# Decode attention, forward and backward: the sums for o and dq with N=512 in four column groups, and the row-broadcast of q in the score bank

## The chip, the cores and the metric

The kernel runs on one core of a Trainium2 chip. The metric is the device time in microseconds; the time before is the median of 12 runs. A profile is one execution, recorded by the hardware profiler. The engines are TensorE (PE; its weight loads are listed as PEld), VectorE (DVE), ScalarE (ACT), GpSimd (POOL) and SyncE (SP); sixteen DMA engines move data between HBM and the on-chip memory (SBUF). Matmul results land in PSUM[...].

## The reference

It is single-query softmax attention for B x H = 64 heads, with Sk = 8192 keys and D = 128, in bf16, together with its gradients:

```python
scores = jnp.einsum("bhqd,bhkd->bhqk", q, k) * scale
p = _softmax(scores, axis=-1)
return jnp.einsum("bhqk,bhkd->bhqd", p, v)
...
_out, _vjp = jax.vjp(_f, q, k, v)
_grads = _vjp(grad_out)
return (_out0, *[jnp.asarray(_g) for _g in _grads])
```

For one head, with s = K q, p = softmax(s) and dp = V g (g is the incoming gradient): o = sum of p_n V_n; dS = p (dp - sum p dp); dq = scale x sum of dS_n K_n; dK_n = scale x dS_n q; dV_n = p_n g. K, V, dK and dV have 2 MB a head each, so a head reads 4 MB and writes 4 MB; o and dq are single rows.

## The kernel before, in words

The 8192 rows of a head are laid out as 128 partitions times NT = 64 row tiles. A loop runs over slots, `SL` = 8 a head and two heads more than there are (L345). In slots 0 to 3 of head i the chunks of 16 tiles of K are transposed on TensorE (`transpose_chunk`, L139) into a PSUM tile `tp` of two banks, and ScalarE copies them to SBUF as `ev` (L147); in slots 4 to 7 the same is done with V. One slot later `score_chunk` (L150) multiplies each transposed tile, as weights, with the column of q (into `sw`) or of g (into `dpw`): 16 matmuls with one column each.

Beside that runs the head before. In slots 0 to 3 `acc_o` (L270) sums E x V: 64 matmuls, each with one column of E as weights and one 128x128 tile of V as the moving operand, into one row `oacc`. In slots 4 to 7 `acc_dq` (L286) sums dS x K: 64 matmuls, each with a tile of K as weights and one column of dS as the moving operand, into one column `qacc`. ScalarE scales the sums (`end_o` L302, `end_dq` L310). VectorE makes dV in slots 2 to 5 and dK in slots 6, 7, 0 and 1 (`outer`, L318: four products of 128x2048 for each), and POOL stores each of them with a DMA (L337) once it is whole.

The softmax's small steps are spread over the slots: maximum along a partition (`max_part`, slot 4), over partitions by a transpose (`max_all`, 5), spread back by a matmul and exponentiated (`max_spread` and `expo`, 6), sum of p x dp (`weigh`, slot 0 of the next head), normalisers, dS and the factors of the outer products (`normalise`, 1). `broadcast` (L108, slot 1) repeats the row of q and that of g over 128 partitions with a matmul and copies the result to `qb`.

Every compute instruction is pinned to program order on its engine. K and V tiles have six buffers of 2 MB (`kvp`). A load is issued by SP (L101, L106) when the sums over the tile that held the buffer are done; outputs have four buffers. PSUM: `tp` 2 x 2 banks, `sw` and `dpw` a bank each, and two banks of the pool `ps_m` that `qbp`, `oacc` and `qacc` share in turn.

Of the kernel before, what the change touches and what calls it, by code (L numbers as in the profile page):

```python
# [8 lines left out]
ACT = mybir.ActivationFunctionType  # L9
ALU = mybir.AluOpType  # L10
AX = mybir.AxisListType
BF16 = mybir.dt.bfloat16
F32 = mybir.dt.float32

CH = 16


@with_exitstack
def kernel(
# [11 lines left out]
    nc = tc.nc  # L31
    B, H, Sq, D = q.shape
    Sk = k.shape[2]
    P = nc.NUM_PARTITIONS
    assert Sq == 1 and D == P
    BH = B * H
    assert BH <= P
    NT = Sk // P
    assert NT * P == Sk and NT == 4 * CH
    NCH = NT // CH  # L40
    SL = 2 * NCH
    scale = float(D) ** -0.5

    load_eng = nc.sync
    store_eng = nc.gpsimd
    pin = tc.keep_in_program_order

    const = ctx.enter_context(tc.tile_pool(name="const", bufs=1))
    kvp = ctx.enter_context(tc.tile_pool(name="kv", bufs=6))
    evp = ctx.enter_context(tc.tile_pool(name="ev", bufs=3))  # L50
    work = ctx.enter_context(tc.tile_pool(name="work", bufs=3))
    outp = ctx.enter_context(tc.tile_pool(name="outp", bufs=4))
    ps_tp = ctx.enter_context(tc.tile_pool(name="ps_tp", bufs=2, space=bass.MemoryType.PSUM))
    ps_sdp = ctx.enter_context(tc.tile_pool(name="ps_sdp", bufs=1, space=bass.MemoryType.PSUM))
    ps_m = ctx.enter_context(tc.tile_pool(name="ps_m", bufs=2, space=bass.MemoryType.PSUM))


    qd_nat = const.tile([BH, 2, D], BF16)
# [9 lines left out]
    ident_bf = const.tile([P, P], BF16)  # L68
# [6 lines left out]

    qdT = const.tile([P, 2, BH], BF16)
    for w in range(2):
        tps = ps_m.tile([P, BH], BF16, tag="m")
        nc.tensor.transpose(tps[:], qd_nat[:, w, :], ident_bf[:BH, :BH])
        nc.vector.tensor_copy(out=qdT[:, w, :], in_=tps[:])  # L80


    dqT = const.tile([P, BH], BF16)
    o_all = const.tile([1, BH, D], BF16)

    class Head:
        pass

    heads = [Head() for _ in range(BH)]

# [17 lines left out]
    def broadcast(i):  # L108

        h = heads[i]  # L110
        qbp = ps_m.tile([P, 2, D], F32, tag="m", name="qbp")
        pin(
            nc.tensor.matmul(  # L113
                qbp[:],
                lhsT=ident_bf[:BH, i : i + 1].to_broadcast([BH, P]),
                rhs=qd_nat[:],
                start=True,
                stop=True,
            )
        )  # L120
        h.qb = work.tile([P, 2, D], BF16, tag="qb", name="qb")
        pin(nc.vector.tensor_copy(out=h.qb[:], in_=qbp[:]))  # L122

    def begin_s(i):

        h = heads[i]
        sw = ps_sdp.tile([P, NT + P + 1], F32, tag="s", name="sw")
        h.s = sw[:, 0:NT]
        h.mT = sw[0:1, NT : NT + P]
        h.mb = sw[:, NT + P : NT + P + 1]  # L130
# [56 lines left out]
    def expo(i):  # L187
        h = heads[i]
        h.E_f = work.tile([P, NT], F32, tag="E_f", name="E_f")
        h.ld = work.tile([P, 2], F32, tag="ld", name="ld")  # L190
        pin(
            nc.scalar.activation(  # L192
                out=h.E_f[:],
                in_=h.s,
                func=ACT.Exp,
                bias=h.negm[:],
                scale=scale,
                accum_out=h.ld[:, 0:1],
            )
        )  # L200
        h.E_bf = work.tile([P, NT], BF16, tag="E_bf", name="E_bf")
        pin(nc.vector.tensor_copy(out=h.E_bf[:], in_=h.E_f[:]))  # L202

    def weigh(i):
        h = heads[i]
# [14 lines left out]
    def normalise(i):  # L220
        h = heads[i]
        pin(nc.tensor.matmul(h.lsum, lhsT=ones_f[:], rhs=h.ld[:], start=True, stop=True))  # L222
        h.rl = work.tile([P, 1], F32, tag="rl", name="rl")
        pin(nc.vector.reciprocal(out=h.rl[:], in_=h.lsum[:, 0:1]))
        negdelta = work.tile([P, 1], F32, tag="negdelta", name="negdelta")
        pin(
            nc.vector.tensor_scalar(
                out=negdelta[:],
                in0=h.lsum[:, 1:2],
                scalar1=h.rl[:],  # L230
                scalar2=-1.0,
                op0=ALU.mult,
                op1=ALU.mult,
            )
        )
        h.rls = work.tile([P, 1], F32, tag="rls", name="rls")
        pin(
            nc.vector.tensor_scalar(
                out=h.rls[:], in0=h.rl[:], scalar1=scale, scalar2=None, op0=ALU.mult
            )  # L240
        )
        dSu = work.tile([P, NT], F32, tag="dSu", name="dSu")
        pin(
            nc.vector.scalar_tensor_tensor(
                out=dSu[:],
                in0=h.dp,
                scalar=negdelta[:],
                in1=h.E_f[:],
                op0=ALU.add,
                op1=ALU.mult,  # L250
            )
        )
        h.dS_bf = work.tile([P, NT], BF16, tag="dS_bf", name="dS_bf")
        pin(nc.vector.tensor_copy(out=h.dS_bf[:], in_=dSu[:]))

        h.pair = []
        for src, norm, tag in ((dSu, h.rls, "ds2"), (h.E_f, h.rl, "p2")):
            d = work.tile([P, NT, 2], BF16, tag=tag, name="pair")
            pin(
                nc.vector.tensor_scalar(  # L260
                    out=d[:],
                    in0=src[:].unsqueeze(2).to_broadcast([P, NT, 2]),
                    scalar1=norm[:],
                    scalar2=None,
                    op0=ALU.mult,
                )
            )
            h.pair.append(d)

    def acc_o(i, c):  # L270

        h = heads[i]
        if c == 0:
            h.oacc = ps_m.tile([1, D], F32, tag="m", name="oacc")
        for n in range(c * CH, (c + 1) * CH):
            pin(
                nc.tensor.matmul(  # L277
                    h.oacc[:],
                    lhsT=h.E_bf[:, n : n + 1],
                    rhs=h.vt[:, n, :],  # L280
                    start=(n == 0),
                    stop=(n == NT - 1),
                )
            )

    def acc_dq(i, c):  # L286

        h = heads[i]
        if c == 0:
            h.qacc = ps_m.tile([P, 1], F32, tag="m", name="qacc")  # L290
        for n in range(c * CH, (c + 1) * CH):
            pin(
                nc.tensor.matmul(  # L293
                    h.qacc[:],
                    lhsT=h.kt[:, n, :],
                    rhs=h.dS_bf[:, n : n + 1],
                    start=(n == 0),
                    stop=(n == NT - 1),
                )
            )  # L300

    def end_o(i):  # L302
        h = heads[i]
        pin(
            nc.scalar.activation(  # L305
                out=o_all[:, i, :], in_=h.oacc[:], func=ACT.Copy, scale=h.rl[0:1, :]
            )
        )

    def end_dq(i):  # L310
        h = heads[i]
        pin(
            nc.scalar.activation(
                out=dqT[:, i : i + 1], in_=h.qacc[:], func=ACT.Copy, scale=h.rls[:]
            )
        )

# [27 lines left out]
    for g in range(SL * (BH + 2)):  # L345
        i, s = divmod(g, SL)
        live = i < BH
        one = 0 <= i - 1 < BH
        two = 0 <= i - 2 < BH

        if s == NCH and 1 <= i and i + 2 < BH:
            load_k(i + 2)
        if s == 0 and 2 <= i and i + 1 < BH:
            load_v(i + 1)
        if live:
            if s == 1:
                begin_s(i)
                broadcast(i)
            if s == NCH + 1:
                begin_dp(i)  # L360
            ev = transpose_chunk(i, s)

        if live and s == 5:
            max_all(i)
        if one and s == 1:
            normalise(i - 1)
        if one:
            if s < NCH:
                acc_o(i - 1, s)
            else:  # L370
                acc_dq(i - 1, s - NCH)
        if live and s == 6:
            max_spread(i)
            expo(i)
        if prev is not None:
            score_chunk(*prev)
        prev = (i, s, ev) if live else None
        if live and s == 4:
            max_part(i)
        if one and s == 0:  # L380
            weigh(i - 1)
        if one and s == NCH - 1:
            end_o(i - 1)
        if one and s == SL - 1:
            end_dq(i - 1)
        if one and 2 <= s < 6:
            outer(i - 1, 1, s - 2)
        if one and s >= 6:
            outer(i - 1, 0, s - 6)
        if two and s < 2:  # L390
            outer(i - 2, 0, s + 2)

    tps = ps_m.tile([BH, P], BF16, tag="m")
    nc.tensor.transpose(tps[:], dqT[:], ident_bf[:])
    dqn = const.tile([BH, D], BF16)
    nc.vector.tensor_copy(out=dqn[:], in_=tps[:])
    load_eng.dma_start(out=out_1.rearrange("b h s d -> (b h s) d"), in_=dqn[:])
    load_eng.dma_start(out=out_0.rearrange("b h s d -> s (b h) d"), in_=o_all[:])


# [28 lines left out]
```

## Time and profile before

| | us |
|---|---|
| median of 12 runs (lowest, highest) | 1329.43 (1322.1, 1336.16) |
| the profiled execution, as timed | 1329.01 |
| its span in the profile | 1327.2 |
| TensorE busy, of it the transposes (L145) | 1215.8, 603.1 |
| o sums (L277), dq sums (L293), TensorE | 298.6, 143.1 |
| ScalarE busy, of it the copies of transposes (L147) | 989.4, 946.1 |
| VectorE busy, of it the outer products (L325) | 744.7, 606.6 |
| a load of V, a store, from issue to landing (median) | 29.4, 26.8 |
| moved by the DMA engines | 540.37 MB, mean 407 GB/s |

Busy time is the time in which an engine executed at least one instruction; since matmuls are pipelined, the mean of one (231 ns for an o matmul) is longer than the distance between two. A timeline line reads: start, duration, engine, line, operation, output <- inputs, shape, number of instructions, and in brackets the idle time before it with what ended it. A line of the table by stage reads: stretch and length, then busy time (and number of instructions) of PE, PEld, DVE, ACT and POOL, the granted TensorE clock, the busy share of the DMA engines, and GB/s. A wait line reads: who waited at which line, for whom at which line, total, times and longest, all in us.

### The profile page before, as it was taken

The page shows a single profiled execution, that of the slowest core. Times are in us where ns is not written, and L with a number is a line of the kernel's source. Part 1 is how long each engine was busy: PE and PEld are TensorE (multiplying, and loading weights), DVE is VectorE, ACT ScalarE, POOL GpSimd, SP SyncE. Part 2 cuts the span into 40 slices and gives each one's busy share as a digit, 9 for nine tenths or more (in the row PEclk, how much of TensorE's full clock was granted, in tenths as well). Part 3 has the DMA queues.
Part 4 walks back from the last instruction along what each step waited for, and adds up shares of the span by engine and source line. Part 5 has one row for each costly group of instructions (what it writes and reads, how often), then busy time and mean ns, then how long its engine had stood idle before and what let it go on. Part 6 is the DMA issues. An engine that isn't in the chain of part 4 may idle for free.

```text
span 1327.2 us, 53368 instructions
## 1 busy us (share of the span) xinstructions
PE 1215.8 (92%) x24963; PEld 1133.3 (85%) x24963; DVE 744.7 (56%) x1412; ACT 989.4 (75%) x769; POOL 69.5 (5%) x136
## 2 busy tenths in 40 slices
PE   7998998899999999998999999999999999998993
PEld 6888897899898889988888888898888888888883
DVE  1555555565665665665565655655555556565655
ACT  7776777777777787877877778777677777776872
POOL 0000000000000000000000000000000000000000
PEclk9888989988989998998988989989789899898997
DMA  9999999999999999999999999999999999999976
GB/s 378 404 388 412 402 413 412 401 379 414 427 415 429 424 425 425 427 425 427 427 414 421 409 414 413 411 421 427 409 407 416 406 409 410 412 386 427 417 320 278
DMA packets 37760, 540.37 MB, mean 407 GB/s; under 512 B 4385, under 2 KB 4385, under 8 KB 4897
## 3 DMA queue, kind: packets, MB, share of 16 engines
q1 hardware_dynamic: 19106, 268.51, 49.1%
q0 software_dynamic: 18432, 268.44, 48.5%
q8 instruction: 195, 3.19, 0.9%
q14 instruction: 27, 0.22, 0.0%
HBM read 268.47 MB, written 268.47 MB: 405 GB/s over the span
## 4 chain that ended last, share of the span: by engine, by line
PE 63%; issue 28%; DMA 5%; POOL 1%; ACT 1%; DVE 0%; SPq 0%; POOLq 0%; ACTq 0%
PE tp L145 28%; PE oacc L277 15%; PE dpw L157 6%; PE sw L157 6%; PE qacc L293 5%; DMA kt<-in_k_dram 4%; POOL out_dram L337 1%; PE sw L179 1%; DMA vt<-in_v_dram 1%; PE qbp L113 1%; PE dpw L222 1%; ACT ev L147 1%; PE sw L173 0%; DVE ob L325 0%; SPq L96 0%
## 5 line engine op out<-in xcount | busy, mean ns | idle before, releaser
L147 ACT COPY ev<-tp 128x2048 bf16<-128x2048 bf16 x512 | 946.1, 1869 | 308.6 <-PE tp L145 304.9
L325 DVE TENSOR_TENSOR ob<-qb,pair 128x2048 bf16<-128x2048 bf16 x512 | 606.6, 1217 | 0.0
L145 PE MATMUL tp<-ident_bf,kt 128*128 128x128 bf16 x4096 | 310.1, 236 | 20.5 <-DMA kt<-in_k_dram 13.4
L145 PE MATMUL tp<-ident_bf,vt 128*128 128x128 bf16 x4096 | 293.0, 228 | 18.1 <-issue 16.7
L277 PE MATMUL oacc<-vt,E_bf 128*1 128x128 bf16 x4096 | 298.6, 231 | 4.2 <-issue 4.1
L157 PEld LDWEIGHTS <-ev 128*128 128x128 bf16 x8192 | 243.6, 97 | 64.9 <-issue 33.3
L145 PEld LDWEIGHTS <-kt 128*128 128x128 bf16 x4096 | 264.5, 106 | 31.5 <-DMA kt<-in_k_dram 14.5
L277 PEld LDWEIGHTS <-E_bf 128*1 128x1 bf16 x4096 | 247.3, 89 | 29.7 <-issue 12.9
L145 PEld LDWEIGHTS <-vt 128*128 128x128 bf16 x4096 | 248.5, 102 | 21.3 <-issue 19.5
L157 PE MATMUL dpw<-qdT,ev 128*128 128x1 bf16 x4096 | 145.4, 164 | 24.5 <-issue 23.1
L293 PE MATMUL qacc<-dS_bf,kt 128*128 128x1 bf16 x4096 | 143.1, 164 | 15.8 <-issue 15.8
L293 PEld LDWEIGHTS <-kt 128*128 128x128 bf16 x4096 | 136.5, 97 | 18.2 <-issue 17.3
L157 PE MATMUL sw<-qdT,ev 128*128 128x1 bf16 x4096 | 141.4, 164 | 3.3 <-issue 2.4
L337 POOL DMA_DIRECT2D out_dram<-ob x128 | 68.4, 534 | 1245.4 <-DVE ob L325 1241.4
L169 DVE TENSOR_REDUCE mp<-sw 128x1 f32<-128x64 f32 x64 | 14.4, 225 | 210.1 <-PE sw L157 210.1
L208 DVE CUSTOM_DVE_ANT_0 junk<-E_f,dpw 128x64 bf16<-128x64 f32 x64 | 14.2, 221 | 169.9 <-PE dpw L157 169.9
L202 DVE CAST E_bf<-E_f 128x64 bf16<-128x64 f32 x64 | 12.5, 195 | 84.1 <-ACT E_f L192 84.1
L182 DVE TENSOR_SCALAR negm<-sw 128x1 f32<-128x1 f32 x64 | 10.1, 159 | 85.0 <-PE sw L179 85.0
L122 DVE CAST qb<-qbp 128x256 bf16<-128x256 f32 x64 | 26.8, 418 | 4.3 <-PE qbp L113 4.3
L179 PE MATMUL sw<-gm,ones_f 1*128 1x1 f32 x128 | 26.1, 270 | 0.9 <-issue 0.9
L305 ACT ACTIVATE o_all<-oacc,rl 1x128 bf16<-1x128 f32 x64 | 22.7, 354 | 4.0 <-PE oacc L277 4.0
L192 ACT ACTIVATE E_f<-sw,negm 128x64 f32<-128x64 f32 x64 | 21.1, 329 | 3.1 <-DVE negm L182 3.0
(34 smaller groups left out, 268.4 us busy)
## 6 DMA issues: line engine op xcount, KB each, us to landing
out_dram<-ob POOLq DMA_DIRECT2D x128, 2048.0 KB, 26.8
vt<-in_v_dram SPq DMA_DIRECT2D x64, 2048.0 KB, 29.4
kt<-in_k_dram SPq DMA_DIRECT2D x63, 2048.0 KB, 27.7
kt<-in_k_dram SPq DMA_DIRECT2D x4, 512.0 KB, 5.3
qd_nat<-in_q_dram SPq DMA_DIRECT2D x1, 16.0 KB, 2.0
qd_nat<-in_grad_out_dram SPq DMA_DIRECT2D x1, 16.0 KB, 2.0
out_dram<-o_all SPq DMA_DIRECT2D x1, 16.0 KB
out_dram<-dqn SPq DMA_DIRECT2D x1, 16.0 KB, 7.2
```

The costliest lines, as they stand in the source:

```text
L122: pin(nc.vector.tensor_copy(out=h.qb[:], in_=qbp[:]))
L145: pin(nc.tensor.transpose(tp[:, t, :], src[:, n0 + t, :], ident_bf[:]))
L147: pin(nc.scalar.copy(out=ev[:], in_=tp[:]))
L157: nc.tensor.matmul(dst[:, n0 + t : n0 + t + 1], lhsT=ev[:, t, :], rhs=qdT[:, w, i : i + 1], start=True, stop=True,)
L169: pin(nc.vector.reduce_max(out=h.mp[:], in_=h.s, axis=AX.X))
L179: pin(nc.tensor.matmul(h.mb, lhsT=ones_f[0:1, :], rhs=h.gm[:], start=True, stop=True))
L192: nc.scalar.activation(out=h.E_f[:], in_=h.s, func=ACT.Exp, bias=h.negm[:], scale=scale, accum_out=h.ld[:, 0:1],)
L277: nc.tensor.matmul(h.oacc[:], lhsT=h.E_bf[:, n : n + 1], rhs=h.vt[:, n, :], start=(n == 0), stop=(n == NT - 1),)
L293: nc.tensor.matmul(h.qacc[:], lhsT=h.kt[:, n, :], rhs=h.dS_bf[:, n : n + 1], start=(n == 0), stop=(n == NT - 1),)
L305: nc.scalar.activation(out=o_all[:, i, :], in_=h.oacc[:], func=ACT.Copy, scale=h.rl[0:1, :])
L325: nc.vector.tensor_tensor(out=h.ob[:, n0 : n0 + CH, :].rearrange("p n (e t) -> p n e t", t=2), in0=h.qb[:, w, :] .rearrange("p (e t) -> p ...
L337: store_eng.dma_start(out=dst[i], in_=h.ob[:])
```

## The change

The sums for dq and o get one form, `acc(i, w, c)`: four row tiles are the moving operand of one matmul (128 x 512), with 32 neighbouring columns of dS or E as weights, of which the first four belong to these tiles. Its output is 32 partitions x 512 fp32. The four matmuls of a chunk write to the four blocks of 32 partitions of one bank, four column groups of the array. So 16 matmuls take the place of 64. In each block only row j of the j-th 128 columns (j from 0 to 3) is wanted. `pick` multiplies the bank by a mask `diag` on VectorE and adds the four parts; `join` adds up the 128 partitions with an fp32 matmul against ones, and ScalarE scales the column. The pick for o stands in slot 4, its join in slot 6; the pick for dq in slot 0 of the next head, its join in slot 2. E and dS are written to padded buffers of 92 columns, three of each, cleared once. o is now collected as columns and transposed at the end, as dq was.

`ps_m` now holds one bank for each of the two sums. The row-broadcast of q and g goes to the free part of the score bank `sw`, and is made in slot 0, ahead of the first transposes of K.

```diff
+QT = 4
+CW = 32
+NG = 4
...
-    ps_m = ctx.enter_context(tc.tile_pool(name="ps_m", bufs=2, space=bass.MemoryType.PSUM))
+    ps_m = ctx.enter_context(tc.tile_pool(name="ps_m", bufs=1, space=bass.MemoryType.PSUM))
...
+    groups = [g * P // NG for g in range(NG)]
+    diag = const.tile([P, QT, D], F32)
+    nc.vector.memset(diag[:], 0.0)
+    for g in groups:
+        nc.vector.tensor_copy(
+            out=diag[g : g + CW],
+            in_=ident_f[g : g + CW, g : g + QT].unsqueeze(2).to_broadcast([CW, QT, D]),
+        )
+
+    NW = NT + CW - QT
+    NBUF = 3
+    E_pads = [const.tile([P, NW], BF16, name=f"E_pad{j}") for j in range(NBUF)]
+    dS_pads = [const.tile([P, NW], BF16, name=f"dS_pad{j}") for j in range(NBUF)]
+    for t in E_pads + dS_pads:
+        nc.vector.memset(t[:], 0.0)
...
-        qbp = ps_m.tile([P, 2, D], F32, tag="m", name="qbp")
...
-                qbp[:],
+                h.qbp,
...
-        sw = ps_sdp.tile([P, NT + P + 1], F32, tag="s", name="sw")
+        sw = ps_sdp.tile([P, NT + P + 1 + 2 * D], F32, tag="s", name="sw")
+        h.qbp = sw[:, NT + P + 1 :].rearrange("p (w d) -> p w d", w=2)
...
-        h.E_bf = work.tile([P, NT], BF16, tag="E_bf", name="E_bf")
-        pin(nc.vector.tensor_copy(out=h.E_bf[:], in_=h.E_f[:]))
+        h.E_bf = E_pads[i % NBUF]
+        pin(nc.vector.tensor_copy(out=h.E_bf[:, 0:NT], in_=h.E_f[:]))
...
-    def acc_o(i, c):
-
-        h = heads[i]
+    def acc(i, w, c):
+
+        h = heads[i]
+        rows = h.vt if w else h.kt
+        wts = h.E_bf if w else h.dS_bf
         if c == 0:
-            h.oacc = ps_m.tile([1, D], F32, tag="m", name="oacc")
-        for n in range(c * CH, (c + 1) * CH):
+            h.acc[w] = ps_m.tile([P, QT * D], F32, tag=f"acc{w}", name="acc")
+        for m in range(CH // QT):
+            n0 = c * CH + m * QT
+            g = groups[m % NG]
             pin(
                 nc.tensor.matmul(
-                    h.oacc[:],
-                    lhsT=h.E_bf[:, n : n + 1],
-                    rhs=h.vt[:, n, :],
-                    start=(n == 0),
-                    stop=(n == NT - 1),
+                    h.acc[w][g : g + CW, :],
+                    lhsT=wts[:, n0 : n0 + CW],
+                    rhs=rows[:, n0 : n0 + QT, :].rearrange("p n d -> p (n d)"),
+                    start=(c == 0 and m < NG),
+                    stop=(c == NCH - 1 and m >= CH // QT - NG),
                 )
             )
...
+    def pick(i, w):
+
+        h = heads[i]
+        full = work.tile([P, QT, D], F32, tag="full", name="full")
+        h.sel = work.tile([P, D], F32, tag="sel", name="sel")
+        NR = P
+        pin(
+            nc.vector.tensor_tensor(
+                out=full[0:NR],
+                in0=h.acc[w][0:NR].rearrange("p (n d) -> p n d", n=QT),
+                in1=diag[0:NR],
+                op=ALU.mult,
+            )
+        )
+        pin(
+            nc.vector.reduce_sum(
+                out=h.sel[0:NR], in_=full[0:NR].rearrange("p n d -> p d n"), axis=AX.X
+            )
+        )
+
+    def join(i, w):
+
+        h = heads[i]
+        NR = P
+        pin(
+            nc.tensor.matmul(
+                h.acc[w][:, 0:1], lhsT=h.sel[0:NR], rhs=ones_f[0:NR, 0:1], start=True, stop=True
+            )
+        )
         pin(
             nc.scalar.activation(
-                out=o_all[:, i, :], in_=h.oacc[:], func=ACT.Copy, scale=h.rl[0:1, :]
-            )
-        )
...
+                out=(oT if w else dqT)[:, i : i + 1],
+                in_=h.acc[w][:, 0:1],
+                func=ACT.Copy,
+                scale=(h.rl if w else h.rls)[:],
             )
         )
...
-            if s == 1:
+            if s == 0:
                 begin_s(i)
                 broadcast(i)
...
-            if s < NCH:
-                acc_o(i - 1, s)
-            else:
-                acc_dq(i - 1, s - NCH)
+            acc(i - 1, 1 if s < NCH else 0, s % NCH)
+        if one and s == NCH + 2:
+            join(i - 1, 1)
+        if two and s == 2:
+            join(i - 2, 0)
...
-        if one and s == NCH - 1:
-            end_o(i - 1)
-        if one and s == SL - 1:
-            end_dq(i - 1)
+        if one and s == NCH:
+            pick(i - 1, 1)
+        if two and s == 0:
+            pick(i - 2, 0)
...
-    load_eng.dma_start(out=out_0.rearrange("b h s d -> s (b h) d"), in_=o_all[:])
+    for w, (src, dst, name) in enumerate(((dqT, out_1, "dqn"), (oT, out_0, "on"))):
+        tps = ps_m.tile([BH, P], BF16, tag=f"acc{w}", name="tps")
+        nc.tensor.transpose(tps[:], src[:], ident_bf[:])
+        nat = const.tile([BH, D], BF16, name=name)
+        nc.vector.tensor_copy(out=nat[:], in_=tps[:])
+        load_eng.dma_start(out=dst.rearrange("b h s d -> (b h s) d"), in_=nat[:])
```

More of the change, by code (lines that the diff above doesn't have):

```diff
@@ L77 @@
     for w in range(2):
-        tps = ps_m.tile([P, BH], BF16, tag="m")
+        tps = ps_m.tile([P, BH], BF16, tag=f"acc{w}", name="tps")
         nc.tensor.transpose(tps[:], qd_nat[:, w, :], ident_bf[:BH, :BH])
@@ L83, with __init__ @@
     dqT = const.tile([P, BH], BF16)
-    o_all = const.tile([1, BH, D], BF16)
+    oT = const.tile([P, BH], BF16)
+    groups = [g * P // NG for g in range(NG)]
[12 more added lines that the diff above has]
+        nc.vector.memset(t[:], 0.0)
     class Head:
-        pass
+        def __init__(self):
+            self.acc = [None, None]
     heads = [Head() for _ in range(BH)]
@@ L121, in broadcast @@
         h.qb = work.tile([P, 2, D], BF16, tag="qb", name="qb")
-        pin(nc.vector.tensor_copy(out=h.qb[:], in_=qbp[:]))
+        pin(nc.vector.tensor_copy(out=h.qb[:], in_=h.qbp))
     def begin_s(i):
         h = heads[i]
-        sw = ps_sdp.tile([P, NT + P + 1], F32, tag="s", name="sw")
+        sw = ps_sdp.tile([P, NT + P + 1 + 2 * D], F32, tag="s", name="sw")
+        h.qbp = sw[:, NT + P + 1 :].rearrange("p (w d) -> p w d", w=2)
         h.s = sw[:, 0:NT]
@@ L252, in normalise @@
         )
-        h.dS_bf = work.tile([P, NT], BF16, tag="dS_bf", name="dS_bf")
-        pin(nc.vector.tensor_copy(out=h.dS_bf[:], in_=dSu[:]))
+        h.dS_bf = dS_pads[i % NBUF]
+        pin(nc.vector.tensor_copy(out=h.dS_bf[:, 0:NT], in_=dSu[:]))
         h.pair = []
@@ L283, in acc_o @@
                 )
             )
-    def acc_dq(i, c):
+    def pick(i, w):
         h = heads[i]
[L289 to L298, printed above, removed]
-                )
-            )
@@ L302, in end_o @@
-    def end_o(i):
-        h = heads[i]
+        full = work.tile([P, QT, D], F32, tag="full", name="full")
[7 more added lines that the diff above has]
+                op=ALU.mult,
+            )
+        )
[4 more added lines that the diff above has]
+        )
@@ L304, in end_o @@
+    def join(i, w):
+        h = heads[i]
+        NR = P
[4 more added lines that the diff above has]
+        )
         pin(
             nc.scalar.activation(
-                out=o_all[:, i, :], in_=h.oacc[:], func=ACT.Copy, scale=h.rl[0:1, :]
-            )
-        )
-    def end_dq(i):
-        h = heads[i]
-        pin(
-            nc.scalar.activation(
-                out=dqT[:, i : i + 1], in_=h.qacc[:], func=ACT.Copy, scale=h.rls[:]
+                out=(oT if w else dqT)[:, i : i + 1],
+                in_=h.acc[w][:, 0:1],
+                func=ACT.Copy,
+                scale=(h.rl if w else h.rls)[:],
@@ L391 @@
             outer(i - 2, 0, s + 2)
[L393 to L397, printed above, removed]
-    load_eng.dma_start(out=out_0.rearrange("b h s d -> s (b h) d"), in_=o_all[:])
+    for w, (src, dst, name) in enumerate(((dqT, out_1, "dqn"), (oT, out_0, "on"))):
[4 more added lines that the diff above has]
+        load_eng.dma_start(out=dst.rearrange("b h s d -> (b h s) d"), in_=nat[:])
 _INS = ['q', 'k', 'v', 'grad_out']
```

## The prediction

> **What bounds the kernel now.** I read the page first: busy times, transfer rate by slice, DMA queues, the chain that ended last.
>
> ```profile
> PE 1215.8 (92%) x24963; PEld 1133.3 (85%) x24963; DVE 744.7 (56%) x1412; ACT 989.4 (75%) x769; POOL 69.5 (5%) x136
> ...
> GB/s 378 404 388 412 402 413 412 401 379 414 427 415 429 424 425 425 427 425 427 427 414 421 409 414 413 411 421 427 409 407 416 406 409 410 412 386 427 417 320 278
> ...
> q1 hardware_dynamic: 19106, 268.51, 49.1%
> q0 software_dynamic: 18432, 268.44, 48.5%
> ...
> PE 63%; issue 28%; DMA 5%; POOL 1%; ACT 1%; DVE 0%; SPq 0%; POOLq 0%; ACTq 0%
> ```
>
> Two things look full at once. TensorE is busy 92% of the span and holds 63% of the chain. But loads (q1) and stores (q0) together took 97.6% of sixteen DMA engines' span, and for ten slices the rate stood at 424 to 429 GB/s as at a ceiling. Which of the two is the limit decides everything, so next the SP queue's own waits and the busy time by stage.
>
> ```profile
> SPq L101 <- PE oacc L277: 690.3, 61, 16.7
> SPq L106 <- PE qacc L293: 502.8, 61, 10.6
> ...
> 60.00:100.00 40.00, 37.63 (x737) 34.86 (x734) 20.89 (x42) 29.58 (x22) 2.13 (x4) 0.85 0.99 392
> ...
> 500.00:600.00 100.00, 97.67 (x2049) 91.64 (x2046) 60.79 (x114) 80.92 (x63) 5.86 (x11) 0.91 1.01 426
> ...
> 1000.00:1100.00 100.00, 92.39 (x1917) 86.39 (x1913) 56.07 (x105) 76.87 (x60) 5.33 (x10) 0.91 1.00 406
> ```
>
> Loads are issued when the sums over V and K free a buffer: that speaks for TensorE. But the last columns (granted clock, DMA share, GB/s) show the engines' share at 0.99 to 1.01 in every stretch. So I looked at when each of the sixteen engines reports its part of a transfer done; the trace has all sixteen marks of nearly every load. The last mark came behind the fifteenth by this much:
>
> ```
> load landed at (us)   305  408  510  613  716  818  920  1023  1127  1230
> last behind 15th (us) 0.5  1.7  4.5  7.2  9.7 12.6 13.1  17.4  16.0  16.9
> ```
>
> The stores show the same ramp. **One DMA engine is slower than the other fifteen.** Nearly all their 16 KB packets take 0.611 us in the plateau; about one packet in sixteen takes 0.62 to 0.70 (by the packet rows around 1287 us, where that engine works alone: about 0.63 a load packet, 0.65 a store packet). A transfer is usable only when its last sixteenth is there, so this engine's pace counts. From 347 us, where its lag is near zero, to 1325 us, where it catches up at the last store, each engine moved 1521 packets: 978/1521 = 0.643 us. A load with a store is 16 packets, 10.3 us; a head (two of each) 20.6 us. Heads start 20.2 us apart on average over all 63 gaps. So from about 350 us on the kernel runs at the pace of one slow engine, and TensorE only looks like the limit: it fills its slack with half-clock stretches (granted clock 0.90). Before 350 us, with no lag, TensorE is the limit: the 527.3 packets of 4 to 347 us took 0.6505 each.
>
> **The change part by part.** One head of TensorE's work at full clock:
>
> ```profile
> 603.08 1.07 PE L145 MATMUL tp<-ident_bf,kt 128*128 128x128 bf16 x16 [0.67 <-DMA kt<-in_k_dram]
> ...
> 608.33 1.05 PE L145 MATMUL tp<-ident_bf,kt 128*128 128x128 bf16 x16
> 609.32 1.05 PE L277 MATMUL oacc<-vt,E_bf 128*1 128x128 bf16 x16
> 610.30 0.55 PE L157 MATMUL sw<-qdT,ev 128*128 128x1 bf16 x16
> 610.72 1.05 PE L145 MATMUL tp<-ident_bf,kt 128*128 128x128 bf16 x16
> ...
> 614.98 1.05 PE L145 MATMUL tp<-ident_bf,vt 128*128 128x128 bf16 x16
> 615.87 0.27 PE L173 MATMUL sw<-ident_f,mp 128*1 128x128 f32 x1
> 615.98 0.54 PE L293 MATMUL qacc<-dS_bf,kt 128*128 128x1 bf16 x16
> 616.38 0.54 PE L157 MATMUL dpw<-qdT,ev 128*128 128x1 bf16 x16
> 616.78 1.05 PE L145 MATMUL tp<-ident_bf,vt 128*128 128x128 bf16 x16
> ...
> 620.39 0.54 PE L157 MATMUL dpw<-qdT,ev 128*128 128x1 bf16 x16
> ```
>
> Start to start: sixteen transposes 0.89, sixteen o matmuls 0.98, sixteen dq matmuls 0.40, sixteen scores 0.41. The whole head runs from 603.08 to about 620.8: 17.7 us.
>
> *Removed:* 4 x 0.98 + 4 x 0.40 = 5.5 us a head.
>
> *Added, 32 matmuls with N=512.* No row has column groups. The nearest is the transposes' pace: 0.89/(16 x 128) = 0.435 ns a column, 0.22 us for 512. If four groups overlap fully, eight groups of four cost about 8 x 0.24 = 1.9 us a head. If nothing overlaps, not even the weight load (row L277: 89 ns for a one-column load), 32 x (0.22 + 0.09) = 10.0 us. The Trainium skill is on both sides. "TensorE: Matmul & The Clock Gate", section "Packing small matmuls — row/col tiling", gives 2.38 times for three column tiles at N=512: as an estimate 0.22 x 3/2.38 = 0.28 us a group, 2.2 us a head. It also says that a weight load is pulled ahead of a running matmul only where the row groups differ; here all use all 128 rows, which would mean 10.0. The trace weighs against that reading: the o matmuls, all rows too, come 61 ns apart (0.98/16), though a weight load (89) and 128 columns (56) make 145 one after the other. I take 2.2. "TensorEngine Tiling (Array Packing)", "Key Properties", speaks against the change: switching the tiling mode drains TensorE. Sixteen switches a head, at the 164 ns that one single-column matmul lasts (row L157), are up to 2.6 us more; no run here shows a switch, so zero to 2.6, and I take 1.3.
>
> *Added, two joins:* fp32 with 128x128 weights, as the L222 pair (0.34 us by its timeline row): 0.7 us a head. Bounds 0.4 and 0.8.
>
> TensorE sum: 17.7 - 5.5 + 2.2 + 1.3 + 0.7 = 16.4 us (14.8 to 23.5 between the ends), against 20.6 for the slow DMA engine. Throttled time comes on top, perhaps 1 to 2 us as now.
>
> *VectorE:* two picks a head, each 512 fp32 products out of PSUM and a reduction of 512. By rows L122 (256 elements, 418 ns) and L202 (64, 195 ns), 1.16 ns an element: 0.72 us and, from L169 (64, 225 ns), 0.75; 1.5 us a pick (1.2 to 1.6). 64 x 2.9 = 188 us, so VectorE goes from 745 to about 930 us, 70%. The o pick stands behind mp and ahead of an outer product and gm in VectorE's order; gm comes about 0.2 + 1.5 + 1.2 + 0.3 = 3.2 us after mp's scores, and TensorE asks for it (L179, behind join) about 3.1 us after them. Free, or a few tenths; uncovered it would be 1.5 us a head. Everything that TensorE has queued behind it, next the scores, would wait with it, and ScalarE's exponential too. The dq pick stands ahead of the reciprocal, which nothing needs until the dq sums three slots on.
>
> *The rest.* ScalarE's two small copies shrink from 354+273 to about 2 x 273 ns; it needs 8 x 1.87 + 1.1 = 16 us a head, inside 20.6. The broadcast moves to slot 0, before K is needed; its bank was last read in slot 6, and its cast only moves ahead of weigh (0.42 us): zero. The setup (a mask, six cleared buffers, some 5 us of VectorE, between nothing and 5) lies beside the first loads. TensorE's instructions fall by a quarter, so instruction fetches too (q8 has 0.9% of the engines): under 3 us, mostly on other engines. Loads and stores are the same; no queue gets another order. At the end three picks make the last store's issue 4 us later (1314.9 to about 1319), but the slow engine is busy with the store before it until 1321: zero.
>
> **Sum.** The slow engine has 2048 packets. About 57 are loads before any store (it has no lag until 41 us): 57 x 0.611 = 34.8. The others, 1991 x 0.643 = 1280.2. With 4 us ahead of the first and 2.2 behind the last: 1321.2 us of span, against 1327.2. So at most 6 us are to be won, all of it where TensorE is the limit now, before 350 us. I take three quarters: span 1322.7. The profiled execution took 1329.01, 1.8 over its span, and the median is 1329.43; so 1324.5 us, 0.37% less.
>
> **Rivals.** *A, the forecast*, 1324.5 (1318 to 1330): the slow engine sets the end. For it: lag ramp and pace. Against: it cannot be seen on the page.
> *B, TensorE is the limit or the slow pace comes from TensorE's load.* Then the plateau's 0.617 mean holds for all: 2048 x 0.617 = 1264, with 4 and 2.2 and some 20 us of a drained end: 1290, and 1.8: about 1292. For it: 63% of the chain, and SP's waits for TensorE. Against: the lag grows just where TensorE is quickest (500 to 600).
> *C, slower: column groups don't overlap and weight loads aren't pulled ahead.* The sums cost 10.0 us, TensorE 17.7 - 5.5 + 10.0 + 0.7 = 22.9, and with 64 x (22.9 - 20.6) = 147 us more the kernel takes about 1475; partial overlap ends anywhere between. It decides from the point where four matmuls take over 20.6 - 12.9 = 7.7 us a head, 0.96 us a group. For it: the row-group rule, the mode switch. Against: the 61 ns pace of the o matmuls.
>
> **Chances.** A 0.65, B 0.12, C 0.23. About 0.3% (4 us) is what a measurement can tell from no change. A's own spread gives faster 0.36, within 0.26, slower 0.03; B is faster; C is within 0.03, slower 0.20. Together 0.48, 0.29, 0.23. For 8 in 10 the range takes A, a quarter of B and half of C: 1305 to 1358; A alone is 1318 to 1330.
>
> **What would show it.** Right: the lag of the last sixteenth ramps from before 150 us on, reaches some 15 us by about 750 us and stays; TensorE's busy time falls to about 1000 us or less while heads stay 20 to 20.6 us apart; TensorE waits for kt and vt loads far more than 15 us in sum. Groups of four acc matmuls start about 0.3 us apart (C: over 0.9). VectorE reads about 930 us. Wrong: packets of the slow engine below 0.63 us, or heads under 20 us apart.

## The result and the profile after

| us | before | after |
|---|---|---|
| median (lowest, highest) | 1328.82 (1322.1, 1336.16), 32 runs | 1305.27 (1303.77, 1308.01), 8 runs |
| the profiled execution: timed, span | 1329.01, 1327.2 | 1309.48, 1307.7 |

The ratio is 0.9825, 95% interval 0.9808 to 0.9841: 23.5 us or 1.8% less. The forecast was 4.9 us less; the direction is right, the size far too small. The profiled execution of after lies 4 us above its median, so the trace has 19.5 of the 23.5 us to account for.

The page of after:

```profile
PE 1158.0 (89%) x19076; PEld 923.6 (71%) x19076; DVE 958.8 (73%) x1680; ACT 984.6 (75%) x769; POOL 69.5 (5%) x136
...
GB/s 375 424 426 426 429 428 426 429 428 427 427 428 428 426 422 424 425 405 426 426 428 422 422 400 430 424 412 406 426 429 411 414 422 418 420 394 420 420 267 263
...
q8 instruction: 149, 2.44, 0.7%
...
issue 51%; DMA 27%; PE 13%; DVE 3%; POOL 3%; ACT 1%; SPq 0%; POOLq 0%; ACTq 0%
```

TensorE has 5,887 instructions less. Its share of the chain fell from 63% to 13% and that of the transfers rose from 5% to 27%. The rate now stands at 424 to 429 GB/s, as in the plateau of before, already from the second slice to the fourteenth. The queue of instruction packets (q8) moved 149; the page of before has this line for it:

```profile
q8 instruction: 195, 3.19, 0.9%
```

The view of waits shows who waits for transfers (waiting engine and line, for whom; total, times, longest). Before:

```profile
PE tp L145 <- DMA kt<-in_k_dram: 13.4, 10, 2.6
...
PE tp L145 <- DMA vt<-in_v_dram: 1.2, 1, 1.2
```

After:

```profile
DVE ob L357 <- DMA out_dram<-ob: 185.5, 104, 2.9
...
PE tp L167 <- DMA vt<-in_v_dram: 73.5, 39, 2.3
...
PE tp L167 <- DMA kt<-in_k_dram: 41.0, 36, 2.5
```

Before, TensorE waited for loads 14.6 us in all, and no wait of VectorE's outer products for a store stood in the view. Now it is 114.5 and 185.5 us. The same by stage, after:

```profile
60.00:100.00 40.00, 39.29 (x762) 31.62 (x761) 36.63 (x63) 38.94 (x32) 3.20 (x6) 1.00 1.01 427
500.00:600.00 100.00, 92.88 (x1483) 74.44 (x1480) 74.72 (x130) 76.33 (x60) 5.33 (x10) 0.77 1.00 419
1000.00:1100.00 100.00, 87.29 (x1508) 69.47 (x1507) 73.71 (x127) 77.23 (x61) 5.33 (x10) 0.90 1.00 417
```

Early (60 to 100 us) it is 427 GB/s at full clock, against 392 before; in the middle the rate is no better than before (419 and 417, against 426 and 406). So most of the gain is early. The starts of the heads (K's first transposes) show it: the first sixteen gaps are 18.54 us in the mean (20.22 before), the later ones 20.29 (20.25 before). The mean of the first sixteen hides a step. The broadcast (L134), once a head, marks the starts in the timeline of after:

```profile
37.17 0.28 PE L134 MATMUL sw<-qd_nat,ident_bf 64*128 64x256 bf16 x1
...
52.77 0.28 PE L134 MATMUL sw<-qd_nat,ident_bf 64*128 64x256 bf16 x1
...
99.55 0.28 PE L134 MATMUL sw<-qd_nat,ident_bf 64*128 64x256 bf16 x1
...
101.50 1.54 PE L167 MATMUL tp<-ident_bf,kt 128*128 128x128 bf16 x16 [1.66 <-DMA kt<-in_k_dram]
```

These heads come 15.6 us apart, at TensorE's own pace. From 101.5 us on TensorE has caught up with the loads and waits for them, and from the eighth head on heads come some 20.3 us apart, as before the change. The last head starts 24.3 us earlier than before (1256.85 against 1281.16); the end after it is 4.9 us longer.

The last of the sixteen completion marks of a load came behind the fifteenth, in after, by this much:

```
load landed at (us)   141  202  303  395  506  608  709  820  901 1003 1104 1206
last behind 15th (us) 0.5  1.5  3.2  5.7  7.7 10.0 12.5 13.8 17.0 15.7 18.1 17.0
```

It is the ramp of before, begun some 160 us earlier. At about 1287 us, when the store issued at 1274.59 has landed, the late sixteenth has caught up and waits for the stores that are still to come. POOL issues the last four so (timeline of after: start, duration, engine, line, operation, tiles, count, idle time before):

```profile
1274.59 0.53 POOL L369 DMA_DIRECT2D out_dram<-ob  x1 [8.67 <-DVE ob L357]
1286.86 0.53 POOL L369 DMA_DIRECT2D out_dram<-ob  x1 [11.73 <-DVE ob L357]
1293.05 0.53 POOL L369 DMA_DIRECT2D out_dram<-ob  x1 [5.66 <-DVE ob L357]
1299.24 0.53 POOL L369 DMA_DIRECT2D out_dram<-ob  x1 [5.66 <-DVE dqn L430]
```

Before, the last three came 4.5 us apart (1305.80, 1310.34, 1314.89); now 6.2, because a pick stands in each gap.

### The profile page after: what moved, and what is told of

Its sections match the earlier page's. It is cut to its first block, busy times and chain, and to the rows that moved or that the text cites. A ratio compares the mean times of both kernels' runs of the same rounds, so it can differ in the third digit from the quotient of the medians.

```text
span 1307.7 us, 41737 instructions
## 1 busy us (share of the span) xinstructions
PE 1158.0 (89%) x19076; PEld 923.6 (71%) x19076; DVE 958.8 (73%) x1680; ACT 984.6 (75%) x769; POOL 69.5 (5%) x136
## 4 chain that ended last, share of the span: by engine, by line
issue 51%; DMA 27%; PE 13%; DVE 3%; POOL 3%; ACT 1%; SPq 0%; POOLq 0%; ACTq 0%
DMA vt<-in_v_dram 20%; PE tp L167 7%; DMA kt<-in_k_dram 5%; POOL out_dram L369 3%; DMA out_dram<-ob 2%; PE acc L303 2%; DVE ob L357 2%; PE dpw L179 1%; PE sw L179 1%; ACT ev L169 1%; DVE sel L327 0%; PE acc L337 0%; PE sw L201 0%; DVE full L319 0%; SPq L118 0%
## 5 line engine op out<-in xcount | busy, mean ns | idle before, releaser
L357 DVE TENSOR_TENSOR ob<-qb,pair 128x2048 bf16<-128x2048 bf16 x512 | 611.7, 1217 | 185.5 <-DMA out_dram<-ob 185.5
L167 PE MATMUL tp<-ident_bf,vt 128*128 128x128 bf16 x4096 | 330.2, 245 | 73.7 <-DMA vt<-in_v_dram 73.5
L167 PEld LDWEIGHTS <-vt 128*128 128x128 bf16 x4096 | 284.4, 111 | 77.5 <-DMA vt<-in_v_dram 76.9
L167 PEld LDWEIGHTS <-kt 128*128 128x128 bf16 x4096 | 281.5, 111 | 52.2 <-DMA kt<-in_k_dram 48.4
L327 DVE TENSOR_REDUCE sel<-full 128x128 f32<-128x512 f32 x128 | 134.3, 1049 | 4.4
L303 PE MATMUL acc<-vt,E_pad 128*32 128x512 bf16 x1024 | 117.4, 449 | 0.0
L303 PE MATMUL acc<-kt,dS_pad 128*32 128x512 bf16 x1024 | 116.4, 446 | 0.9 <-DVE dS_pad L276 0.9
L319 DVE TENSOR_TENSOR full<-acc,diag 128x512 f32<-128x512 f32 x128 | 87.6, 684 | 0.0
L337 PEld LDWEIGHTS acc<-ones_f,sel 128*128 128x128 f32 x256 | 42.8, 210 | 44.0 <-issue 24.1
L337 PE MATMUL acc<-ones_f,sel 128*128 128x1 f32 x256 | 53.7, 279 | 8.9 <-DVE sel L327 8.8
L303 PEld LDWEIGHTS <-dS_pad 128*32 128x32 bf16 x1024 | 26.7, 95 | 38.8 <-issue 20.8
L244 PEld LDWEIGHTS dpw<-ld,ones_f 128*128 128x128 f32 x128 | 23.4, 228 | 10.1 <-DVE ld L230 9.8
```

The source lines that it names most:

```text
L167: pin(nc.tensor.transpose(tp[:, t, :], src[:, n0 + t, :], ident_bf[:]))
L303: nc.tensor.matmul(h.acc[w][g : g + CW, :], lhsT=wts[:, n0 : n0 + CW], rhs=rows[:, n0 : n0 + QT, :].rearrange("p n d -> p (n d)"), start=( ...
L319: nc.vector.tensor_tensor(out=full[0:NR], in0=h.acc[w][0:NR].rearrange("p (n d) -> p n d", n=QT), in1=diag[0:NR], op=ALU.mult,)
L327: nc.vector.reduce_sum(out=h.sel[0:NR], in_=full[0:NR].rearrange("p n d -> p d n"), axis=AX.X)
L337: nc.tensor.matmul(h.acc[w][:, 0:1], lhsT=h.sel[0:NR], rhs=ones_f[0:NR, 0:1], start=True, stop=True)
L357: nc.vector.tensor_tensor(out=h.ob[:, n0 : n0 + CH, :].rearrange("p n (e t) -> p n e t", t=2), in0=h.qb[:, w, :] .rearrange("p (e t) -> p ...
```

## The experiments

Two theories had to be told apart. **Pace by itself** (the forecast): one DMA engine is slow whatever the kernel computes. **Pace from the load**: something that TensorE does slows it; its fetching of instructions, its time, or its traffic with SBUF. All edits are against the changed kernel; the ratios are to the kernel before, measured beside each of them.

**Loads and stores only:**

```diff
...
-    for g in range(SL * (BH + 2)):
...
+    for i in range(BH):
+        load_k(i)
+        load_v(i)
+        store_eng.dma_start(out=dv_v[i], in_=heads[i].vt[:])
+        store_eng.dma_start(out=dk_v[i], in_=heads[i].kt[:])
...
```

> Loads and stores alone, same sizes, queues and buffers: every K and V tile is loaded and stored again as dK and dV, and q and grad_out are written as o and dq; all computation is left out. It gives the floor of the transfers. If one DMA engine is slow by itself (theory 1 and 2): the last sixteenth of a transfer lags again, packets of that engine at 0.62 to 0.64 us, and 4 + 2048 x 0.63 = about 1295 (1280 to 1305). If the slow engine is slow only because of what the compute engines do: no lag, packets of 0.611 everywhere, 4 + 1251 + 4 = about 1260.

1256.16 us, ratio 0.9436 (0.9407 to 0.9465). Its page:

```profile
span 1255.0 us, 585 instructions
...
GB/s 362 429 432 432 431 431 429 432 433 430 431 433 430 431 430 431 434 430 431 432 430 433 430 431 433 430 431 431 430 433 429 431 433 431 431 430 432 433 430 367
```

Between the first slice and the last the rate stays at 429 to 434 GB/s, and the last mark is never more than 1.9 us late. No DMA engine is slow by itself: the first theory falls, and with it the floor of 1321 us. The same bytes can move in 1255.

**Stores issued by SP instead of POOL:**

```diff
-    store_eng = nc.gpsimd
+    store_eng = nc.sync
```

> The changed kernel with the stores issued by SP, on the queue of the loads, in place of POOL. If the slow DMA engine is slow because of POOL's queue (the Trainium skill, DMA: Bandwidth & Descriptors, Latency and other measured facts, guesses at that queue's descriptor rings), the lag of the last sixteenth goes away and packets are 0.611 everywhere: 1285 to 1295. If it is slow by itself: 1305 or more. Against both: SP issues in order, so a load can stand behind a store that waits for VectorE; up to 1 us of emptier queues a head, 1310 to 1370.

1308.70 us, ratio 0.9833 (0.9804 to 0.9862): the time of after. A lag still grows, though it spreads: the last mark gets up to 8.8 us behind the fifteenth, and the fifteenth up to 13.8 us behind the eighth, so several engines are late. POOL's queue may bear on which engines are late, but it is not what costs the time. For this kernel that speaks against a guess in the Trainium skill, "DMA: Bandwidth & Descriptors", section "Latency and other measured facts", which puts the slowness of two DMA engines down to the descriptor rings of such queues, as its best guess.

**96 tiny matmuls more a head,** to add instructions without much work:

```diff
...
             ev = transpose_chunk(i, s)
+            for _ in range(24 if s < NCH else 0):
+                pin(
+                    nc.tensor.matmul(
+                        heads[i].junk1, lhsT=qdT[:, 0, 0:1], rhs=qdT[:, 1, 0:1], start=True, stop=True
+                    )
+                )
```

> The changed kernel with 96 more matmuls a head (24 in each of slots 0 to 3), one weight column and one moving column each, into an unused element of the score bank. They bring TensorE's instruction count back to that of the kernel before (about 25000 matmuls), while the large reads of SBUF stay as in the changed kernel. Theory 1 (the slow DMA engine's packets got shorter, 0.643 to about 0.636 us, because a quarter of the instruction fetches fell away): its store packets go from about 643 back to about 655 ns, and the time from 1305 to about 1318. Theory 2 (they got shorter because TensorE reads less, or because of something else in the new sums): packets stay at 643 and 628 ns, time 1305 to 1308. If TensorE's own time were the limit: 96 x 25 to 60 ns = 2.4 to 5.8 us a head, 1340 or more, with waits of TensorE for loads falling from 115 us to near nothing.

1530.55 us, ratio 1.1484 (1.142 to 1.1548), far more than the two theories of the transfers had. TensorE was busy 94%, hardly a lag was left (at most 2.9 us), and the clock fell to 0.72: TensorE became the limit, the third case of the expectation. A group of small matmuls and the next instruction in the timeline of this kernel:

```profile
613.73 0.74 PE L397 MATMUL sw<-qdT 128*1 128x1 bf16 x24
614.40 0.40 PE L245 MATMUL dpw<-ld,ones_f 128*128 128x2 f32 x2
```

That is 0.67 us, 2.7 us a head, 172 us in all; the small matmuls also stood behind the cast of `qb`, in the bank that they wrote to (54.9 us of waits). Together this is about the 225 us lost: none of it fell into slack. It says nothing on fetching.

**All four groups on the same 32 columns** (the four matmuls of a chunk go to one block of the bank; nothing is left out):

```diff
-NG = 4
+NG = 1
...
-    groups = [g * P // NG for g in range(NG)]
+    groups = [g * CW for g in range(NG)]
...
-        NR = P
+        NR = NG * CW
```

> The changed kernel with all four matmuls of a chunk in the same column group (NG = 1), one after the other into the same 32 partitions; picks and joins then run on 32 partitions. It measures what the overlap of column groups is worth. Groups of four should take 4 x 0.22 = 0.9 us in place of 0.33. If TensorE has slack (DMA theory), 8 x 0.57 = 4.6 us a head more brings it from about 16 to about 21 us, just over the 20.3 us of the slow DMA engine: 1310 to 1350. If TensorE is the limit already: 1305 + 64 x 4.6 = about 1600.

1334.51 us, ratio 1.0027 (1.0014 to 1.004). The page and the timeline of this kernel:

```profile
PE 1307.4 (98%) x19076; PEld 904.1 (68%) x19076; DVE 952.0 (71%) x1677; ACT 996.6 (75%) x769; POOL 69.2 (5%) x136
```

```profile
602.86 1.04 PE L303 MATMUL acc<-kt,dS_pad 128*32 128x512 bf16 x4
603.83 0.55 PE L179 MATMUL sw<-qdT,ev 128*128 128x1 bf16 x16
```

Start to start, four matmuls take 0.97 us here. In the changed kernel (timeline of after, four column groups and a join):

```profile
608.62 0.40 PE L303 MATMUL acc<-vt,E_pad 128*32 128x512 bf16 x4
608.95 0.55 PE L179 MATMUL dpw<-qdT,ev 128*128 128x1 bf16 x16
...
613.00 0.38 PE L337 MATMUL acc<-ones_f,sel 128*128 128x1 f32 x2
613.24 0.54 PE L179 MATMUL sw<-qdT,ev 128*128 128x1 bf16 x16
```

0.33 us: the groups overlap, 2.9 times faster. Without that, 8 x 0.64 = 5.1 us a head come back, 328 us in all, of which 29 reach the end. TensorE is then 98% busy at a granted clock of 0.994, and the lag is gone (at most 3.3 us). So the overlap of the column groups is what the change stands on: with as few instructions, but without it, nothing is won. This is only half of rival C, in which weight loads were not hidden either; here they are (0.97/4 = 0.24 us a matmul, 0.31 in C). At 0.97 us a group the kernel stands just where C was to begin to decide (0.96), and the time is that of before. C's 1475 was not put to the test.

The next runs ask what slows a sixteenth of the transfers. Three add one kind of load to the loads and stores alone, tied to nothing; each of the three ran once. (The four runs of loads and stores alone lie within 1.2 us.) **SBUF traffic without TensorE:** 1000 products on VectorE and 640 copies on ScalarE, 128x2048 bf16 each:

```diff
...
+    for _ in range(1000):
+        pin(nc.vector.tensor_tensor(out=vb[:], in0=va[:], in1=va[:], op=ALU.mult))
+    for _ in range(640):
+        pin(nc.scalar.copy(out=vd[:], in_=vc[:]))
...
```

> Loads and stores alone, and beside them 1000 products of 128x2048 bf16 on VectorE and 640 copies of 128x2048 bf16 on ScalarE, SBUF to SBUF, with almost no instructions to fetch. Fetch theory: no lag, 1256 to 1262. Traffic theory, VectorE and ScalarE: lag and packets of 0.62 to 0.70 us, 1280 to 1310.

1270.56 us, but only because these two engines work longer than the transfers, which ended at 1256.3. Its page:

```profile
PE 0.5 (0%) x2; PEld 0.2 (0%) x2; DVE 1231.7 (97%) x1016; ACT 1216.0 (96%) x641; POOL 69.3 (5%) x136
```

The two engines are busy 97 and 96%, and no last mark is more than 3.3 us behind the fifteenth: their traffic costs the transfers 3.5 us.

**22,000 matmuls of full size:**

```diff
...
+    for _ in range(22000):
+        pin(nc.tensor.matmul(mmp[:], lhsT=ident_bf[:], rhs=ident_bf[:], start=True, stop=True))
...
```

> The same with full operands: 22000 matmuls with 128x128 weights and 128 moving columns, all from SBUF, at the same rate. Fetch theory: the same lag and time as the run with one-row operands. Traffic theory, TensorE's reads: lag and packets of 0.62 to 0.70 us here and not there.

1308.08 us; the transfers ended at 1304.2. The page:

```profile
span 1306.3 us, 44585 instructions
...
q8 instruction: 172, 2.82, 0.8%
...
L375 PE MATMUL mmp<-ident_bf 128*128 128x128 bf16 x22000 | 1231.1, 219 | 0.0
```

TensorE's matmuls alone bring the lag of the loads back (7.5 us at 371, about 26 at 1000), and the time of the whole kernel with it.

**22,000 matmuls of one weight, on one partition:**

```diff
...
+    for _ in range(22000):
+        pin(nc.tensor.matmul(mmp[0:1, :], lhsT=ident_bf[0:1, 0:1], rhs=ident_bf[0:1, :], start=True, stop=True))
...
```

> Loads and stores alone (no computation of the attention), and beside them, tied to nothing, 22000 matmuls on TensorE with one row and one column of weights and one row of 128 moving elements: about 56 ns each, so instructions are fetched at the rate of the kernel before (some 14 packets in 100 us), and hardly any SBUF is read. Fetch theory (each instruction packet delays a data packet by some 0.36 us, mostly on one engine; 195 of them make 0.611 into 0.645 us there, 149 make 0.637): the lag of the last sixteenth comes back, up to about 2% while TensorE runs, and the time is 1290 to 1320. Theory of SBUF traffic (TensorE, VectorE and ScalarE slow the engine's packets): no lag, 1256 to 1262.

The expectation was wrong on their pace: each took 107 ns, not 56, so TensorE ran until 2351 us, long after the transfers. The page:

```profile
GB/s 393 430 430 429 429 429 430 429 430 430 429 429 426 420 426 427 424 424 425 425 425 226 1 1 1 1 1 1 1 1 1 1 1 1 1 1 1 1 1 1
...
L375 PE MATMUL mmp<-ident_bf 1*1 1x128 bf16 x22000 | 2346.8, 309 | 0.0
```

The miss makes it the more telling. While the transfers ran, to 1279.7 us, TensorE was busy all the time as in the run before, but it had come through about half as many instructions, and 93 instruction packets had been fetched. The lag of the loads grew to about 21 us. Beside each other (lag: of the last mark of a load behind the fifteenth):

```
                       transfers ended  instruction packets  largest lag
                              (us)         till then           (us)
transfers only               1252.8            0                1.9
+ VectorE, ScalarE           1256.3            0                3.3
+ matmuls 1x1                1279.7           93               21.7
+ matmuls 128x128            1304.2          172               29.6
after                        1305.6          149               19.4
before                       1325.0          195               18.0
```

(1279.7 - 1252.8)/93 = 0.29 us and (1304.2 - 1252.8)/172 = 0.30 us a packet. TensorE's busy time until then is the same to about 5%, and the data that it reads differs by more than a hundredfold; the delay follows neither, but the number of instructions, and with it that of the packets that bring them. In the two kernels with the same work beside them, 0.30 us a packet make a floor of 1252.8 + 195 x 0.30 = 1311.3 before and 1252.8 + 149 x 0.30 = 1297.5 after; they end 13.7 and 8.1 us above it.

**Only o in the new form,** dq summed as before, so that one part of the change is there with half of the saving in instructions:

```diff
+            if s < NCH:
+                acc(i - 1, 1, s)
+            else:
+                acc_dq(i - 1, s - NCH)
...
-        if two and s == 2:
-            join(i - 2, 0)
...
-        if two and s == 0:
-            pick(i - 2, 0)
+        if one and s == SL - 1:
+            end_dq(i - 1)
```

> One part alone: the o sums in the new form, the dq sums as before (64 matmuls with a tile of K as weights), with one pick and one join a head, broadcast in the score bank. TensorE 17.7 - 3.9 + 1.3 + 0.35 = 15.5 us a head, below the changed kernel's; matmuls a head 336 against 288 there and 384 before. Fetch theory: about 172 instruction packets, slow engine at 0.641 us, so about 1311, 5 us slower than the changed kernel. If the gain is TensorE's time (or VectorE's work costs): 1300 to 1305, not slower than the changed kernel.

1311.59 us, ratio 0.9865 (0.9829 to 0.99), with 172 instruction packets: 0.30 x 23 = 6.9 us above after by the price, 6.3 by the medians. But the two ratios' intervals overlap, and the ends of the transfers in the two traces are only 2.0 us apart (1307.6 and 1305.6). It agrees with the theory and does not prove it. Most of the gain is there with one sum alone.

## Why the prediction was right and where it was wrong

**The range held by luck.** 1305.27 us lies 0.3 us inside the stated 1305 to 1358, and the low end was there only for a part of rival B; the forecast alone had 1318 to 1330. The measured time is nearer to B's 1292 than to the forecast's 1324.5, and it came by a mechanism that is neither's as it stands.

**Transfers, not TensorE, are what is left: right.** The signs named ahead are there: the lag is 0.5 us at 141 us, 12.5 at 709 and about 17 from 901 on, heads from the seventeenth on start 20.29 us apart, and TensorE waits for loads 114.5 us. A group takes 0.33 us from start to start, as forecast (about 0.3). A sign named for being wrong came too: the first heads start 15.6 us apart, under the 20 of the forecast.

**"TensorE only looks like the limit", already before, from 350 us on: only half right.** Heads came 20.25 us apart, while the late sixteenth needed 32 x 0.643 = 20.6. It fell behind some 16 us and hardly anything waited for it (TensorE for loads 14.6 us in all), since loads lead by several buffers. TensorE set the pace of the heads, and the late sixteenth came due at the end: the last store, issued at 1314.89, landed 10.1 us later, against 6.4 in the kernel without a lag (one group). The two limits lay about 4 us apart. After the change the late sixteenth also sets the pace.

**The step that failed is "the others, 1991 x 0.643 = 1280.2", the slow engine's pace carried over unchanged,** and behind it "so instruction fetches too (q8 has 0.9% of the engines): under 3 us, mostly on other engines". After the change these packets took 1305.6 - 38.8 = 1266.8 us, of which 3.2 were spent idle at the end: 0.635 each, 1264 us and not 1280.2. The pace isn't that of an engine; it comes with TensorE's instructions. 46 packets fewer, at the price of the experiments, are 46 x 0.30 = 13.8 us on the very sixteenth that ends last. As an estimate, after with the packets of before would end its transfers at 1305.6 + 13.8 = 1319.4; the forecast's floor without the 2.2 us behind the last packet is 1319.0. That the two agree so well is partly chance: 13.8 us of the 19.4 is what the price explains, and the start and the end, below, miss in opposite directions. Rival B had the cause on the right side (the pace comes from TensorE), at 1292 too low: the slow pace doesn't vanish, it falls with the quarter of the instructions that went.

The packets of the late sixteenth show when the time was won. Before, it had done 527.3 by 347 us. After, the mean engine had done 555 and the late one, 4.4 us behind, about 548; to 1287 us it did 1476 more, 940/1476 = 0.637 each; the last 24 took 18.6 us. Early: (548 - 527.3) x 0.643 = 13.3 us. Middle: 1476 x 0.006 = 9. End: 24 x 0.643 - 18.6 = -3.2. Together 19, of 19.4 that the transfers end earlier.

**Where the gain would be, before 350 us: the place right, the size wrong.** The forecast had at most 6 us there, since 0.643 was to hold from 41 us on; 0.628 was reached ((347 - 38.8)/(548 - 57)).

**The tail at zero: wrong.** From the start of the last head to the end of the span it is 50.9 us, against 46.0. The late sixteenth ran dry at about 1287 us, so nothing covered the picks any more: the last two joins waited for them, 4.0 and 4.8 us. And from 1267 us on TensorE ran at half clock, so the last four slots took 12 us instead of 7. In the steady state picks are free, as forecast: the view of waits has no other wait of a join's matmul for a pick.

**TensorE's sum: a little too high.** A group took 0.33 us with all drains, 8 x 0.33 = 2.6 us a head where 2.2 + 1.3 had been taken, and a join 0.24 to 0.31, so some 0.5 for two where it was 0.7. With 17.7 - 5.5 + 2.6 + 0.5 a head has 15.3 us of work, not 16.4; the first heads came 15.6 apart. (The ends given for the sum, 14.8 to 23.5, are not what the terms' ends make: 12.2 + 1.9 + 0.4 = 14.5 and 12.2 + 10.0 + 2.6 + 0.8 = 25.6. Nothing rests on them.) Busy time is 1158 us and not "1000 or less": 0.826 of the clock was granted, against 0.900. Work at half clock takes about twice as long (sixteen transposes 1.7 to 1.8 us near 1270 us in after, 0.9 at full clock), so busy time was a poor sign.

**VectorE: right in effect, 3% too low.** Product and reduction by the page of after:

```profile
L327 DVE TENSOR_REDUCE sel<-full 128x128 f32<-128x512 f32 x128 | 134.3, 1049 | 4.4
...
L319 DVE TENSOR_TENSOR full<-acc,diag 128x512 f32<-128x512 f32 x128 | 87.6, 684 | 0.0
```

0.72 was forecast for the product and 0.75 for the reduction, which took 1.05. It reads four strided parts, unlike the row from which it was taken; whether that is the reason was not tried. Busy 958.8 us, 930 forecast.

**What stays open.** Whether it is the fetched packet or something else that goes with each TensorE instruction: no run separates the two. How one packet of 16 KB delays one engine by 0.30 us while most others keep 0.611 us a packet, and why the ramp is gentler before 300 us: packet rows don't name the engine. (An instruction packet lasts 0.96 us by its rows in after; if a third of them ran on the late engine, that would make the price. This is an estimate.) Why the clock was granted at 0.72 with the tiny matmuls and at 0.994 with one group. The broadcast put back to its old slot alone, and the last stores cut in quarters against the dry end, were not tried. No complete kernel tried was faster than after.

## What to carry to other kernels

Where transfers run near their ceiling, time the loads and stores alone first: here they took 1256 us where the forecast had taken 1321 for a floor. Compare the last completion mark of a transfer with the one before it; a ramp means that one engine is late, and the mean rate doesn't show it. Then count instructions, not only their time: where transfers set the pace, each 16 KB of TensorE's instructions went with 0.30 us of delay here, so fewer and larger matmuls can pay beyond TensorE's own time.

## What the runs showed of the hardware that was not expected

- With each instruction packet of TensorE the sixteenth of a transfer that ends last comes about 0.30 us later (by 93 and by 172 packets; packet or instructions, that is open). Traffic of VectorE and ScalarE, busy 96 and 97%, costs it 3.5 us in all.
- Four matmuls of 512 columns on four column groups take 0.33 us, on one group 0.97 (0.24 each). In the second case, too, the weight loads are hidden, although all rows are used. "TensorE: Matmul & The Clock Gate", section "Packing small matmuls — row/col tiling", has 2.38 times for three groups; for four it was 2.9 times here, between matmuls on the whole array.
- Matmuls with one weight on one partition and 128 columns took 107 ns each, twice as long as 128x128 ones (1231.1 us/22000 = 56 ns). Sixteen 128x128 transposes in a half-clock stretch of after take 1.66 us (from 1269.78), 104 ns each: half clock throughout may be the reason. The trace of that run has no record of the granted clock, so it is not shown.
- 328 us more of TensorE time (one group) cost 29 us: the waits and half-clock stretches that the quicker kernel had (granted clock 0.826) were filled first. But 172 us more in tiny matmuls, with 55 of waits, cost 225 us, at a clock of 0.72: time at half clock is not slack as such.
